# A gated linear attention followed by a SwiGLU: the norm's roots spread over the partitions by way of DRAM, and the column sum of the squares in four column groups

## The chip, the cores and the metric

The kernel runs on one core of a Trainium2 chip. The metric is the device time of one execution in microseconds. The core has TensorE (PE in the profile; its weight loads are shown apart as PEld), VectorE (DVE), ScalarE (ACT), GpSimd (POOL) and SyncE (SP), which here only issues DMAs.

## The reference

Four sequences of 768 steps and eight heads of 48 features go through a recurrent attention with a complex gate (`gateloop`); its output, with the heads side by side as 3072 tokens of 384 features, goes through an RMS norm and a SwiGLU of width 1536.

```python
mag = np.sqrt(a_re * a_re + a_im * a_im)
scale = np.minimum(mag, 0.999) / (mag + 1e-06)
a_re_n, a_im_n = (a_re * scale, a_im * scale)
for t in range(S):
    ar, ai = (a_re_n[:, :, t, :, None], a_im_n[:, :, t, :, None])
    new_re = ar * S_re - ai * S_im
    new_im = ar * S_im + ai * S_re
    kv = np.einsum('bhd,bhe->bhde', k[:, :, t], v[:, :, t])
    S_re, S_im = (new_re + kv, new_im)
    y[:, :, t] = np.einsum('bhd,bhde->bhe', q[:, :, t], S_re)
...
rms = np.sqrt(np.mean(x * x, axis=-1, keepdims=True) + 1e-06)
xn = x / rms * rms_g
g = xn @ w_gate
silu = g * (1.0 / (1.0 + np.exp(-g)))
val = xn @ w_val
return (silu * val @ w_out).astype(np.float32)
```

All data is fp32, and so are all products on TensorE.

## The kernel before

**Tiling.** The 3072 tokens are 24 chunks of C = 128 (n = 0 to 23, six to a sequence). Two chunks make a group (g = 0 to 11) for the feed-forward part. Features lie on the partitions from the attention's output on: `yT` is 3 blocks of 128 features by 128 tokens in one PSUM bank.

**Stages.** `gates(u)` turns the gates of one or two chunks into running products (magnitude and angle) on ScalarE and VectorE and writes the rotated q and k into `rot`; twelve DMAs for two chunks (`kq<-rot`) bring them into the layout `kq`, 96 partitions by head and time. `attend(n)` is the attention of one chunk: score products in column groups of 32 (`bank<-kq`), a masked copy into `am` by VectorE, the products for y (`bank<-am,ve` and `bank<-kq,state`, in column groups too), transposes of k (`bank<-ident,kq`), and the new state (`bank<-vn,kt`, column groups). At its end stands the norm of that chunk. `feed(g, xT)` is the SwiGLU of a group: six pairs of gate and value products (`bank<-xT,wg`, `bank<-xT,wv`, 128x256), ScalarE's Silu into `sg`, VectorE's product into `hT`, and the output products: of 384 columns (`bank<-wo,hT`) for groups 0 and 1, and from group 2 on (`FIRST`) a product of two-by-two blocks with seven instead of eight multiplications, of 192 columns (tiles `wo`, `sums`, `hT`, with sums on VectorE in `mid` and `hT`), into `ot` and by DMA to `out`.

**The norm of a chunk.** ScalarE squares `yT` into `sq`; VectorE multiplies `yT` by the norm's weights into `yg` and adds the three blocks of `sq` into the first (for chunks 0 to 3, whose units are in `LIGHT`, ScalarE does the former, and the three blocks are added by the product). Then, on one column of bank 7:

- the column sum: `sq` as weights, a column of ones as the moving side, so that each token's sum of squares lands on its own partition (`bank<-ones,sq`, 128x1);
- `ssv`: mean and epsilon, on VectorE;
- `rs`: to the power -1/2, on GpSimd (`pow`), 128x1;
- the root product: `rs` widened to 128 columns as weights, the identity as moving side, which puts the 128 roots side by side on every partition (`bank<-ident,rs`, 128x128);
- `xT` = `yg` times that row, on VectorE. `xT` is what the gate and value products of the group read.

**What sets the order.** Every operation is recorded with an estimated duration and what it reads and writes, and `Flow.schedule` makes one list of it: at each step it takes the engine that can start first and on it the ready operation that is due first. Products of the feed-forward part have due times from a running clock; others inherit them from who uses them. A DMA counts as landed 2.0 us after its turn in its queue, and SP has at most eight DMAs under way (`LANES`). A change between products on the whole array and in column groups (`mode=BLK`) counts 0.06 us. Within an engine the order is then fixed; all instructions are issued by one line, L667, so that in the profile groups are told apart by tiles alone. Column groups are seen in the form: `128*128` is the whole array, `128*32` and `96*32` are column groups of 32. One fp32 product of the program leaves two records in the trace.

PSUM: banks 0 to 3 take turns for the feed-forward part, 4 and 5 hold scores and state, 6 holds `yT`, 7 holds the norm's column and row and transposes.

Of the kernel before, what the change touches and what calls it, by code (L numbers as in the profile page):

```python
# [8 lines left out]
FP32 = mybir.dt.float32  # L9
# [7 lines left out]
DRAM = bass.MemoryType.DRAM  # L17

P = 128
C = 128  # L20
BLK = 32
# [440 lines left out]
class Flow:  # L462
# [59 lines left out]
    def add(self, eng, calls, dur, reads=(), writes=(), table=None, land=None, due=None, after=(), behind=(), late=None, mode=None):  # L522
        op = dict(i=len(self.ops), eng=eng, calls=calls, dur=dur, deps=set(), table=table, land=land,
                  base=due, late=late, mode=mode, stage=self.stage, behind={o["i"] for o in behind})
        self.ops.append(op)
        op["deps"].update(o["i"] for o in after)
        for ap in reads:
            self.note(op, ap, False)
        for ap in writes:
            self.note(op, ap, True)  # L530
        return op
# [138 lines left out]
def fast(tc, ctx, qT, kT, v, a_re, a_im, w_gate, w_val, w_out, rms_g, out, H, bad):  # L670
# [6 lines left out]
    N = B * NCH  # L677
# [15 lines left out]

    mem = ctx.enter_context(tc.tile_pool(name="mem", bufs=1))
    psum = ctx.enter_context(tc.tile_pool(name="psum", bufs=1, space=PSUM))
    rooms = {}

    def room(name, shape, dtype=FP32):
        t = mem.tile(shape, dtype, name=name, tag=name)
        row = 1  # L700
        for x in shape[1:]:
            row *= x
        rooms[t.tensor.name] = (name, row * mybir.dt.size(dtype))
        keep.append(t)
        return t

    outside = {x.tensor.name for x in (qT, kT, v, a_re, a_im, w_gate, w_val, w_out, rms_g, out)}
    keep = []
    banks = []
    for i in range(8):  # L710
        t = psum.tile([P, 512], FP32, name=f"bank{i}", tag=f"bank{i}")
# [52 lines left out]
    def act(o, x, func, scale=None, bias=None, accum=None, **kw):  # L764
        k = {}
        if scale is not None:
            k["scale"] = scale
        if bias is not None:
            k["bias"] = bias
        if accum is not None:  # L770
            k["accum_out"] = accum
        dur = 0.17 + 0.86e-3 * cols(o) + 0.09 * len(aps(scale, bias)) + (0.19 if accum is not None else 0.0)
        return add("ACT", [(nc.scalar.activation, (), dict(out=o, in_=x, func=func, **k))], dur,
                   aps(x, scale, bias), aps(o, accum), table=TABLE.get(func), **kw)
# [3 lines left out]
    def run(x):  # L778
        n = 1
        for step, size in reversed([tuple(y) for y in x.ap][0 if x.tensor.name in outside else 1:]):  # L780
            if step != n:
                break
            n *= size
        return n

    def dma(o, x, eng="SP", **kw):
        n = mybir.dt.size(o.dtype)
        for s in o.shape:
            n *= s
        row = mybir.dt.size(o.dtype) * min(run(o), run(x))  # L790
        load = n / row * (0.006 + 50.3e-6 * row) / 16
        op = add(eng, [(QUEUE[eng].dma_start, (), dict(out=o, in_=x))], 0.85 if eng == "POOL" else 0.62, [x], [o],
                 land=2.0 + 1.4 * load, **kw)
        op["load"] = load
        op["packet"] = max(0.07, 0.006 + 50.3e-6 * row * (2 if eng == "POOL" and row == 2048 else 1))
        return op

    def mms(list_, dur, **kw):
        calls, reads, writes = [], [], []
        for o, l, r, start, stop in list_:  # L800
            calls.append((nc.tensor.matmul, (o,), dict(lhsT=l, rhs=r, start=start, stop=stop)))
            reads += [l, r]
            writes.append(o)
        return add("PE", calls, dur, reads, writes, **kw)
# [9 lines left out]
    ident = room("ident", [P, P])  # L814
    causal = room("causal", [C, 2, C])
    mhalf = room("mhalf", [P, 1])
    ones = room("ones", [P, 1])
# [31 lines left out]
    ygs = [room(f"yg{i}", [P, ND, C]) for i in range(2)]  # L849
    ssv = room("ssv", [P, N])  # L850
    rss = [room(f"rs{i}", [P, 1]) for i in range(2)]
    sgs = [room(f"sg{i}", [P, 512]) for i in range(2)]
    ots = [room(f"ot{i}", [C, DM]) for i in range(2)]
    sums = room("sums", [P, 2, HD * DH])
# [106 lines left out]
    EARLY = {0: -100.0, 1: -98.0}  # L961
    SUMMED = ()
    LIGHT = (0, 1, 2)
    turn = {}
    moved = {}
    HOLD = 1
# [134 lines left out]
    def attend(n):  # L1101
# [12 lines left out]
        for a in range(2):  # L1114
            ps = banks[4 + a]
            s = ps.rearrange("s (h t) -> s h t", h=HH)
            list_ = []
            for h in range(HH):
                for b in range(4):
                    c = 3 - b if h % 2 else b  # L1120
# [5 lines left out]
            o = am[:, a * HH:(a + 1) * HH]  # L1126
# [3 lines left out]
        ps = banks[6]  # L1130
# [3 lines left out]
        for i in range(4 * ND):  # L1134
            j, c = divmod(i, 4)
            m, r = divmod(i, 3)
            o = yT[c * BLK:(c + 1) * BLK, j]
# [10 lines left out]
        if not last:  # L1148
            kt = kts[0]
            for a in range(2):  # L1150
                ps = banks[7 - 3 * a]
# [5 lines left out]
            ps = banks[5][0:D2, 0:DM]  # L1157
# [4 lines left out]
            u, i = unit_of[n], n - UNITS[unit_of[n]][0]  # L1162
# [9 lines left out]
        sq, yg = sqs[0], ygs[n % 2]  # L1172
        act(sq, yT, AF.Square)
        if unit_of[n] in LIGHT:
            for j in range(ND):
                act(yg[:, j], yT[:, j], AF.Copy, scale=gcol[:, j:j + 1])
        else:
# [3 lines left out]
        ps = banks[7]  # L1181
        col = ps[:, C:C + 1]
        parts = range(ND if unit_of[n] in LIGHT else 1)
        mms([(col, sq[:, j], ones, j == 0, j == parts[-1]) for j in parts], 0.25 * len(parts))
        sv = ssv[:, n:n + 1]
        ts(sv, col, 1.0 / DM, EPS_RMS, ALU.mult, ALU.add)
        add("POOL", [(nc.gpsimd.tensor_tensor, (), dict(out=rss[n % 2], in0=sv, in1=mhalf,
                                                        op=ALU.pow))], 0.9, [sv, mhalf], [rss[n % 2]])
        wide = ps[:, 0:C]
        mms([(wide, rss[n % 2].to_broadcast([P, P]), ident, True, True)], 0.25)  # L1190
        g = group_of[n]
        ns = GROUPS[g]
        x, lo = xplace[g]
# [2 lines left out]
        i = n - ns[0]  # L1196
# [106 lines left out]
    for n in range(N):  # L1303
        while gated < NU and UNITS[gated][0] <= n:
            gates(gated)
            gated += 1
        xT = attend(n)
        if n == GROUPS[group_of[n]][-1]:
            feed(group_of[n], xT)
            if group_of[n] == 2:  # L1310
                for i in range(len(looks)):
                    look(i)
# [8 lines left out]
    o = 0  # L1321
# [8 lines left out]
    ps = banks[7]  # L1330
# [15 lines left out]
def gateloop_swiglu(tc, qT, kT, v, a_re, a_im, w_gate, w_val, w_out, rms_g, out, H):  # L1346
    nc = tc.nc
    with tc.tile_pool(name="flag", bufs=1) as flag:
        bad = flag.tile([1, 1], I32, name="bad")
        with ExitStack() as ctx:  # L1350
            fast(tc, ctx, qT, kT, v, a_re, a_im, w_gate, w_val, w_out, rms_g, out, H, bad)
        with tc.If(nc.values_load(bad[0:1, 0:1]) > 0):
            general(tc, qT, kT, v, a_re, a_im, w_gate, w_val, w_out, rms_g, out, H)
# [39 lines left out]
```

## Time and profile before

| | |
|---|---|
| time, three runs | 727.68, 730.59, 731.40 us; median 730.59 |
| profiled execution | 729.62 us, span 727.9 us, granted clock 0.99 |
| TensorE busy | 685.7 us (94%), 6906 records |
| VectorE, ScalarE, GpSimd busy | 471.6 (65%), 334.1 (46%), 42.0 us (6%) |
| root products (`bank<-ident,rs`) | 48 records, 10.3 us busy |
| column sums (`bank<-ones,sq`) | 64 records, 9.4 us busy |
| roots on GpSimd (`rs<-ssv,mhalf`) | 24, mean 717 ns |
| xT on VectorE (`xT<-yg,bank`) | 24, mean 547 ns, waited 5.3 us |

The span is from the first to the last instruction of one execution. Busy time of TensorE counts records whose ends are modelled and which overlap, so the mean of a record is longer than its share of the time; the start of one row of the timeline to the start of the next is a better measure. In the page, slices are fortieths of the span, digits tenths; the chain is the work that ended last, followed back from the end.

### The profile page before, as it was taken

How to read it: one execution, taken by the hardware profiler on the slowest of the kernel's cores; microseconds unless marked ns; L12 is line 12 of the kernel's file. 1: busy time of each engine (PE TensorE's matmuls, PEld its weight loads, DVE VectorE, ACT ScalarE, POOL GpSimd, SP SyncE). 2: the span in 40 equal slices, each digit the busy share in tenths (PEclk: the TensorE clock that was granted, in tenths of full speed). 3: DMA queues.
4: the chain of work that ended last, by engine and by line, in shares of the span. 5: the costliest groups of instructions: out<-in, count | busy, mean ns of one | idle time of the engine just before them, and what ended most of it. 6: DMA issues, size and time to landing. Idle time of an engine off the chain costs nothing.

```text
span 727.9 us, 16198 instructions
## 1 busy us (share of the span) xinstructions
PE 685.7 (94%) x6906; PEld 603.7 (83%) x6906; DVE 471.6 (65%) x740; ACT 334.1 (46%) x452; POOL 42.0 (6%) x80
## 2 busy tenths in 40 slices
PE   0579999999999999999999999999999999999996
PEld 0558867877899889889899889889889889889885
DVE  6979988789897887787847737756745234134121
ACT  7649756755656765732923823822821110110010
POOL 6123100001000000000000000000000000000000
PEclk9979999999999999999999999999999999999999
DMA  8797655634545435543722303314303102200000
GB/s 285 226 304 208 193 168 170 184 106 130 170 127 147 153 93 131 171 153 99 189 82 62 97 20 91 97 34 106 81 17 73 55 12 68 65 13 2 23 1 26
DMA packets 104575, 80.64 MB, mean 111 GB/s; under 512 B 42800, under 2 KB 95280, under 8 KB 104496
## 3 DMA queue, kind: packets, MB, share of 16 engines
q1 hardware_dynamic: 100432, 64.99, 32.8%
q0 software_dynamic: 3264, 14.16, 5.5%
q8 instruction: 56, 0.92, 0.5%
q10 hardware_dynamic: 800, 0.39, 0.2%
q14 instruction: 23, 0.19, 0.1%
HBM read 55.84 MB, written 4.72 MB: 83 GB/s over the span
## 4 chain that ended last, share of the span: by engine, by line
PE 87%; DVE 5%; DMA 3%; ACT 2%; SPq 1%; issue 1%; POOL 0%; DVEq 0%; ACTq 0%
PE bank L667 87%; DMA kq<-rot 2%; SPq L667 1%; DVE turns L667 1%; DVE rot L667 1%; DVE wg L667 1%; ACT t L667 1%; DMA in<-in_a_re_dram 1%; ACT turns L667 0%; DVE t L667 0%; DVE wo L667 0%; DVE wv L667 0%; ACT L667 0%; DVE ot L667 0%; DVE in L667 0%
## 5 line engine op out<-in xcount | busy, mean ns | idle before, releaser
L667 PE MATMUL bank<-xT,wg 128*128 128x256 f32 x864 | 199.8, 381 | 1.6 <-DVE xT L667 1.5
L667 PE MATMUL bank<-xT,wv 128*128 128x256 f32 x864 | 199.1, 380 | 0.0
L667 PEld LDWEIGHTS bank<-xT,wg 128*128 128x128 f32 x864 | 163.7, 191 | 24.5 <-DVE xT L667 2.2
L667 PEld LDWEIGHTS bank<-xT,wv 128*128 128x128 f32 x864 | 163.5, 190 | 22.5
L667 PE MATMUL bank<-wo,hT 128*128 128x192 f32 (+1 forms) x576 | 125.8, 362 | 0.4 <-DVE hT L667 0.4
L667 DVE TENSOR_TENSOR hT<-bank,sg 128x512 f32<-128x512 f32 x72 | 49.6, 689 | 114.4 <-PE bank L667 102.0
L667 PEld LDWEIGHTS bank<-wo,hT 128*128 128x128 f32 x576 | 95.6, 191 | 13.7 <-issue 2.5
L667 ACT ACTIVATE sg<-bank 128x512 f32<-128x512 f32 x72 | 42.9, 596 | 132.0 <-PE bank L667 131.4
L667 ACT ACT_TABLE_LOAD x69 | 88.5, 1283 | 11.5 <-DVE rot L667 7.9
L667 ACT ACTIVATE sq<-bank 128x384 f32<-128x384 f32 x24 | 11.8, 490 | 101.2 <-PE bank L667 101.2
L667 DVE TENSOR_TENSOR rot<-kin,turns 128x768 f32<-128x768 f32 x48 | 44.8, 953 | 14.9 <-DMA kq<-rot 14.5
L667 POOL TENSOR_TENSOR rs<-ssv,mhalf 128x1 f32<-128x1 f32 x24 | 17.2, 717 | 575.4 <-DVE ssv L667 575.4
L667 ACT ACTIVATE kt<-bank 128x384 f32<-128x384 f32 x40 | 18.4, 488 | 60.0 <-PE bank L667 59.8
L667 PE MATMUL bank<-sums,hT 128*128 128x192 f32 x240 | 45.0, 329 | 0.0
L667 ACT ACTIVATE turns<-in 128x768 f32<-128x768 f32 (+1 forms) x39 | 29.9, 789 | 21.0 <-DVE rot L667 12.5
L667 PEld LDWEIGHTS bank<-sums,hT 128*128 128x128 f32 x240 | 39.5, 190 | 0.0
L667 PEld LDWEIGHTS bank<-kq 96*32 96x32 f32 x1536 | 30.3, 111 | 10.4 <-issue 7.7
L667 DVE COPY_PREDICATED am<-causal,bank 128x512 f32<-128x512 int32 x48 | 33.3, 722 | 8.4 <-PE bank L667 8.4
L667 DVE TENSOR_TENSOR hT<-hT 128x768 f32<-128x768 f32 x40 | 38.2, 954 | 0.9
L667 PE MATMUL bank<-am,ve 128*32 128x128 f32 x768 | 38.1, 281 | 0.0
L667 PE MATMUL bank<-kq 96*32 96x96 f32 (+3 forms) x1536 | 34.7, 238 | 3.6 <-DMA kq<-rot 3.6
L667 PE MATMUL bank<-rot 128*128 128x128 f32 x64 | 11.7, 342 | 24.8 <-DVE rot L667 24.8
(112 smaller groups left out, 750.5 us busy)
## 6 DMA issues: line engine op xcount, KB each, us to landing
kq<-rot SPq DMA_DIRECT2D x144, 128.0 KB, 2.4
kin<-in_q_dram SPq DMA_DIRECT2D x24, 192.0 KB, 2.8
kin<-in_k_dram SPq DMA_DIRECT2D x24, 192.0 KB, 3.6
wo<-in_w_gate_dram SPq DMA_DIRECT2D x6, 768.0 KB, 4.6
out_dram<-ot SPq DMA_DIRECT2D x24, 192.0 KB, 2.3
wo<-in_w_val_dram SPq DMA_DIRECT2D x6, 768.0 KB, 5.7
wo<-in_w_out_dram SPq DMA_DIRECT2D x6, 768.0 KB, 5.4
in<-in_a_re_dram SPq DMA_DIRECT2D x11, 384.0 KB, 4.6
```

What stands on the lines that cost most here:

```text
L667: fn(*args, **kw)
```

## The change

Two things are changed in the norm. The column sum is cut into four products, each with 32 columns of `sq` as weights, which write 32 partitions each in column groups; in the planner it counts 0.1 us instead of 0.25. For chunks 4 to 21 (`SENT`) the root product is left out: one DMA writes the column `rs` into a line of 128 numbers in DRAM (two such lines take turns), and a second one reads this line into all 128 partitions of a new tile `row` in SBUF (there is one). `xT` is then multiplied by `row` instead of the bank. Chunks 0 to 3, 22 and 23 keep the root product; its estimate in the planner is 0.28 instead of 0.25. Since the planner makes the whole order from such estimates, the order of the other work changes too.

```diff
+    dram = ctx.enter_context(tc.tile_pool(name="dram", bufs=1, space=DRAM))
...
+    lines_ = []
+    for i in range(2):
+        t = dram.tile([1, P], FP32, name=f"line{i}", tag=f"line{i}")
...
+    row = room("row", [P, C])
...
+    SENT = range(4, N - 2)
...
         ps = banks[7]
         col = ps[:, C:C + 1]
         parts = range(ND if unit_of[n] in LIGHT else 1)
-        mms([(col, sq[:, j], ones, j == 0, j == parts[-1]) for j in parts], 0.25 * len(parts))
+        mms([(col[c * BLK:(c + 1) * BLK], sq[:, j, c * BLK:(c + 1) * BLK], ones, j == 0, j == parts[-1])
+             for j in parts for c in range(4)], 0.1 * len(parts), mode=BLK)
         sv = ssv[:, n:n + 1]
         ts(sv, col, 1.0 / DM, EPS_RMS, ALU.mult, ALU.add)
         add("POOL", [(nc.gpsimd.tensor_tensor, (), dict(out=rss[n % 2], in0=sv, in1=mhalf,
                                                         op=ALU.pow))], 0.9, [sv, mhalf], [rss[n % 2]])
-        wide = ps[:, 0:C]
-        mms([(wide, rss[n % 2].to_broadcast([P, P]), ident, True, True)], 0.25)
+        if n in SENT:
+            line = lines_[n % 2]
+            dma(line.rearrange("o t -> t o"), rss[n % 2])
+            wide = row
+            dma(wide, line.to_broadcast([P, C]))
+        else:
+            wide = ps[:, 0:C]
+            mms([(wide, rss[n % 2].to_broadcast([P, P]), ident, True, True)], 0.28)
...
         tt(xT[:, :, i * C:(i + 1) * C], yg, wide.unsqueeze(1).to_broadcast([P, ND, C]))
```

More of the change, by code (lines that the diff above doesn't have):

```diff
@@ L708, in fast @@
     keep = []
+    lines_ = []
+    for i in range(2):
+        t = dram.tile([1, P], FP32, name=f"line{i}", tag=f"line{i}")
+        rooms[t.tensor.name] = (f"line{i}", P * 4)
+        outside.add(t.tensor.name)
+        keep.append(t)
+        lines_.append(t)
     banks = []
```

## The prediction

> **What bounds the kernel now.** I read the page first: busy shares, the span in 40 slices, the chain that ended last.
>
> ```profile
> span 727.9 us, 16198 instructions
> PE 685.7 (94%) x6906; PEld 603.7 (83%) x6906; DVE 471.6 (65%) x740; ACT 334.1 (46%) x452; POOL 42.0 (6%) x80
> ...
> PE   0579999999999999999999999999999999999996
> ...
> PE 87%; DVE 5%; DMA 3%; ACT 2%; SPq 1%; issue 1%; POOL 0%; DVEq 0%; ACTq 0%
> ```
>
> After the first three slices (some 55 us) TensorE never rests, and 87% of the chain is its products. In stretches of 50 us, PE is busy 50.00 us in six of the eleven from 150 to 700 and over 49.1 in the others; its waits over 0.2 us after 120 us are 0.82 (at 324), 0.26 (at 510), 0.89 (at 675) and 0.41 us (at 717), 2.4 together. So here a nanosecond of TensorE is a nanosecond of span, and other engines matter only if they make TensorE wait. Busy time says little of pipelined products, so I price them by starts, in the timeline of PE. A column "x6" counts records; one fp32 product of the program leaves two.
>
> ```profile
> 314.51 0.88 PE L667 MATMUL bank<-vn,kt 128*32 128x48 f32 x48
> 315.30 0.77 PE L667 MATMUL bank<-kq 96*32 96x128 f32 x32
> ...
> 333.72 1.14 PE L667 MATMUL bank<-sums,hT 128*128 128x192 f32 x6
> 334.79 0.43 PE L667 MATMUL bank<-am,ve 128*32 128x128 f32 x8
> 335.03 0.40 PE L667 MATMUL bank<-kq,state 96*32 96x128 f32 x8
> ...
> 336.35 0.40 PE L667 MATMUL bank<-kq,state 96*32 96x128 f32 x8
> 336.69 1.24 PE L667 MATMUL bank<-hT 128*128 128x192 f32 x6
> 337.76 0.38 PE L667 MATMUL bank<-ident,rs 128*128 128x128 f32 x2
> 337.99 1.14 PE L667 MATMUL bank<-wo,hT 128*128 128x192 f32 x6
> 338.96 1.14 PE L667 MATMUL bank<-sums,hT 128*128 128x192 f32 x6
> 339.94 0.28 PE L667 MATMUL bank<-ones,sq 128*128 128x1 f32 x2
> 340.08 1.22 PE L667 MATMUL bank<-sums,hT 128*128 128x192 f32 x6
> 341.14 1.14 PE L667 MATMUL bank<-wo,hT 128*128 128x192 f32 x6
> ```
>
> Four prices stand in these starts. Six records of 192 columns that nothing disturbs take 0.97 us (337.99 to 338.96). **A root product** (ident,rs) takes 0.23 (337.76 to 337.99). **A column sum** (ones,sq) takes 0.14, and the six records behind it 1.06 instead of 0.97: 0.23 here, 0.20 as a mean over all of them; I take 0.21. **A visit to column groups** (from 128*128 to a form in *32 and back) costs time besides its products: the six records before it take 1.07 (+0.10), its first eight 0.24 and its last eight 0.34 where an inner eight take 0.22 (+0.02, +0.12), the six after it 1.07 (+0.10). That is 0.34 here; the same subtraction over all visits between 120 and 715 us gives 0.31, so 0.155 for each change of mode. **A record in column groups** takes 16.5 ns at 48 columns (0.79 us by 48) and 27.5 ns at 128 (0.22 by 8).
>
> **The change, part by part.** The schedule that the program makes for itself is known before it runs: I compared the order of instructions of both kernels on each engine.
>
> *Roots.* 18 of 24 root products go (chunks 4 to 21): 18 x 0.23 = -4.1 us, all on the path.
>
> *Column sums.* Two of the first chunks fall into time in which PE waits anyway and are left out. Before, 20 sums of one part and 2 of three: 26 x 0.21 = 5.4 us. After, a part is four products, 8 records: 26 x 8 = 208 records. No record of the trace moves one column in column groups; the nearest, at 48 columns, is 16.5 ns and falls with the columns, so I take 15: 3.1 us. Ends: 10 ns (2.1) and the 27.5 of 128 columns (5.7). So -2.3, between -3.3 and +0.3.
>
> The Trainium skill, "TensorEngine Tiling (Array Packing)", section Instruction Overhead, speaks against this part: a product of one column lasts as long as one of 60, and a small dimension should not be tiled. At its 60 cycles, 25 ns at 2.4 GHz (an estimate from that page, with the clock of the page "TensorE: Matmul & The Clock Gate"), the part would give -0.2 and not -2.3; the 16.5 ns at 48 columns are already below that, so the row decides.
>
> *Changes of mode.* The order holds 120 changes between the two modes before and 150 after. In 22 of 24 chunks the new sum stands alone between products of the whole array: 44 changes, and 14 fall away because the order is another elsewhere. Without the two visits in the early wait it is 26 x 0.155 = +4.0 us (26 x 0.17 = 4.4 by the visit shown above).
>
> Sum on PE: -4.1 - 2.3 + 4.0 = **-2.4 us**; with the ends of the column price -3.4 and +0.6 (with 4.4 for the mode). A term nearly cancels a term: what the new sums save goes into visits to the other mode, and the gain is about half of what the roots free.
>
> *DMAs.* 36 issues on SP at 0.6 us each (the SPq pieces of the chain in order of time) are 22 us of SP; SP waited 178 us for PE alone, so its time is there, but not its order. The pow of POOL stays. The multiplication into xT reads SBUF for PSUM: state in 96x384 takes 549 ns from SBUF and 550 from PSUM, so nothing. What counts is the latency, and no row shows a column going to DRAM or a row coming back to all partitions. The nearest:
>
> ```profile
> kq<-rot SPq DMA_DIRECT2D x144, 128.0 KB, 2.4
> out_dram<-ot SPq DMA_DIRECT2D x24, 192.0 KB, 2.3
> ve<-in_v_dram SPq DMA_DIRECT2D x96, 24.0 KB, 2.3
> decay<-ends SPq DMA_DIRECT2D x66, 1.0 KB, 1.8
> ```
>
> The last column is the median from issue to landing. decay<-ends also moves a few bytes for each of 128 places, within SBUF: I take its 1.8 us for the column, 2.4 for the row (64 KB, between ve and kq), 4.2 together; ends 3.6 (twice decay) and, by the latest ve (11.9) behind large loads, over 10. The chain from column sum to feed is then 0.15 (ssv) + 0.55 (pow) + 1.8 + 2.4 + 0.55 (xT) + six handovers of 0.05 = 5.8 us; some 1.5 more where DVE or SP is busy. **The cover:** in the new order the second chunk's sum is followed by 18 output products, 8 transposes and 12 output products before the first gate product of its group, 30 x 2 x 0.163 + 1.3 = 11 us, in eight of nine groups. In the group of chunks 4 and 5 it is 12 products of 384 columns and 16 small ones, 8.4 us. So some 4 us of slack remain, 1 to 2.5 in that first group; I put 0 to 1.5 us of wait there and take 0.2. If the cover goes, each microsecond of lateness is one of span for that group.
>
> *New waits.* On DVE, xT of the first chunk waits for `row`; right behind it in most groups stand the second chunk's ssv, the `mid` additions and the evictions of output products. On SP, `line` waits for the pow and `row` for the landing of `line`; behind them stand kq<-rot and decay (score products of the next chunk need them), loads of k, q, v and `out`. Those are issued well ahead: PE waited for kq only 3.6 us, before 101 us. There is one `row`: a second chunk's read waits for the first's xT. Taken as nothing at the prices above.
>
> *Stalls freed.* Of PE's 2.4 us of waits those at 675 and 717 belong to the last group, whose chunks keep the product; 0.82 and 0.26 may go or move: nothing taken, -1.1 as the end.
>
> Sum: -2.4 + 0.2 = **-2.2 us**. The profiled execution took 729.62 us (span 727.9, 1.7 around it), so 727.4; the median of 730.59 is 0.97 above that execution, so 728.4. Half a per cent, about what a measurement of this kernel can tell from no change, is 3.7 us: the forecast lies inside it.
>
> **The rivals.** *The round trip through DRAM becomes the path (slower).* The two DMAs of both chunks of a group stand almost in series, since DVE runs the second ssv behind the first xT. Let each DMA land D later than assumed; a group then loses 4D less its slack, some 5 us with the little that the first chunk has, and there are nine. It decides from D = 1.2: at 1.5 (column 3.3, row 3.9) it is 9 x 1 = +9 us, 736; at 2, +27. For it: the column is 128 pieces of 4 bytes to one place in DRAM, and single DMAs in the trace land after 5 us and more when behind loads of 768 KB on the same queue. Against: decay at 1.8, and in the second half the queues are nearly empty. Chance 0.2. The Trainium skill, "DMA: Bandwidth & Descriptors", section Specifications, says that pieces below 512 B are read, modified and written; no price stands there and no row of this trace shows it for DRAM.
>
> *The column groups cost more than the roots give (slower or even).* If a one-column record takes the 27.5 ns of 128 columns and a visit 0.34, the sum is +0.6; with 2 to 3 us of waits at the feeds +3 to +4, 733 to 734. Chance 0.06.
>
> *The new order frees more than the sum (faster).* Planned further ahead, the attention of a group ends earlier, the waits at 324 and 510 go, and a record costs 10 ns: -3.4 - 1.1 = -4.5, 726; fewer late drains make it up to -6. Chance 0.14.
>
> That the change does nothing of what it says is excluded by the order: 18 root products are gone and 36 DMAs stand on SP.
>
> **How the numbers follow.** The forecast's case, 0.60, runs from -4 to +2 around -2.2: 0.10 of it is faster by over 0.5%, 0.48 within, 0.02 slower. With the rivals: faster 0.10 + 0.14 = 0.24; same 0.48; slower 0.02 + 0.20 + 0.06 = 0.28. The forecast's own range is 726.5 to 732; the whole reaches from 725 (the faster rival's middle and below left out, 0.08) to 738 (D above 1.6 left out, some 0.12).
>
> **What would show it.** Right: 12 records of ident,rs (6 products); 256 of ones,sq (32 parts by 8) in a form *32 with starts 10 to 20 ns apart; 0.3 us lost around each lone sum; `line` landing in about 2 us, `row` in about 2.4; no wait of PE for xT over 0.5 us outside the first and last groups. Wrong: PE waiting for xT in most groups (the DRAM rival), landings over 3 us, starts of 25 ns and more in the sums, or a visit that costs well under or over 0.31.

## The result and the profile after

The changed kernel takes 857.49 us (median of four runs) against 729.94 before: 1.1753 times as long, 95% interval 1.1687 to 1.182. The forecast was 728.4 us with a range to 738. The rival "the round trip through DRAM becomes the path" is what happened: 127.6 us, where it was worked out for 9 (each DMA 1.5 us late) and 27 (2 us late).

The page of the changed kernel, busy time, slices and chain:

```profile
span 852.9 us, 16622 instructions
...
PE 717.7 (84%) x7066; PEld 623.2 (73%) x7066; DVE 471.0 (55%) x740; ACT 330.5 (39%) x449; POOL 46.1 (5%) x80
...
PE   0679899769959968987994997996798799699996
...
PEclk9999999979979989996997998998899799799999
...
PE bank L667 17%; DMA line<-rs 3%; SPq L667 1%; DMA row<-line 1%; DMA kq<-rot 1%; DVE hT L667 0%; DVE ot L667 0%; DVE xT L667 0%; DVE mid L667 0%; DVE ssv L667 0%; DVEq L667 0%
```

Three things are new: TensorE has holes through the whole middle of the run; its granted clock, full after the start before, now dips beside them; and `line<-rs` and `row<-line` stand in the chain. The chain's shares stop at a quarter of the span because it could be followed back no further, so they are not a breakdown. Who waited for whom says more:

```profile
DVE xT L667 <- DMA row<-line: 149.3, 18, 11.3
...
PE bank L667 <- DVE hT L667: 38.8, 9, 9.3
...
PE bank L667 <- DVE ot L667: 24.3, 6, 6.1
```

(total, times, longest.) All 18 rows were waited for, 8.3 us each on VectorE. TensorE waited in turn, and mostly not for `xT` itself (9.9 us in all) but for what stood behind it on VectorE: output evictions (`ot`) and sums for the output products (`hT`). The DMA issues of the changed kernel, KB each and median us from issue to landing:

```profile
kq<-rot SPq DMA_DIRECT2D x144, 128.0 KB, 3.5
...
row<-line SPq DMA_DIRECT2D x18, 64.0 KB, 4.6
...
line<-rs SPq DMA_DIRECT2D x18, 0.5 KB, 7.9
```

The column of 512 bytes takes 7.9 us where 1.8 was assumed, the row 4.6 where 2.4 was: 12.5 for the round trip instead of 4.2. (The page gives a landing for 8 of the columns and 10 of the rows; from the semaphores' updates, as in e4 below, the 18 columns take 6.9 to 9.8 us and the 18 rows 4.0 to 5.4.) `kq<-rot`, at 2.4 us before, lands in 3.5: traffic behind the new DMAs on the queue is later too. By the same updates, a `kq<-rot` issued while a column is under way takes 6.4 us at the median, while a row is under way 4.5, and otherwise still 2.4. One group (chunks 12 and 13) shows how that becomes time. VectorE's timeline (start, us, engine, operation, idle before it and who ended that):

```profile
434.33 0.16 DVE L667 TENSOR_SCALAR ssv<-bank 128x1 f32<-128x1 f32 x1 [0.35 <-PE bank L667]
...
450.14 0.56 DVE L667 TENSOR_TENSOR xT<-yg,row 128x384 f32<-128x384 f32 x1 [9.81 <-DMA row<-line]
450.61 0.15 DVE L667 TENSOR_SCALAR ssv<-bank 128x1 f32<-128x1 f32 x1
...
463.87 0.56 DVE L667 TENSOR_TENSOR xT<-yg,row 128x384 f32<-128x384 f32 x1 [8.89 <-DMA row<-line]
...
466.20 0.55 DVE L667 TENSOR_TENSOR ot<-bank,mid 128x384 f32<-128x384 f32 x1
```

SyncE's in the same stretch:

```profile
437.20 0.53 SPq L667 DMA_DIRECT2D line<-rs  x1
...
445.28 0.33 SPq L667 DMA_DIRECT2D row<-line  x1
...
451.66 0.33 SPq L667 DMA_DIRECT2D line<-rs  x1
...
458.62 0.33 SPq L667 DMA_DIRECT2D row<-line  x1
```

And TensorE's:

```profile
450.82 0.55 PE L667 MATMUL bank<-ident,kq 96*128 96x96 f32 x4 [3.44 <-DVE ssv L667]
454.50 2.29 PE L667 MATMUL bank<-wo,hT 128*128 128x192 f32 x6 [3.13 <-DVE hT L667]
...
466.81 1.65 PE L667 MATMUL bank<-xT,wg 128*128 128x256 f32 x3 [6.09 <-DVE ot L667]
```

The two round trips are in series, as the rival said: the second chunk's column sum was done on TensorE at 441, but its `ssv` stands behind the first `xT` on VectorE (450.61), so the second column goes out at 451.66. Between 447 and 467 TensorE loses 12.7 us in these three waits. The first product after them, a transpose into bank 7, waits for `ssv` because it needs the bank that `ssv` reads. The wait at 466.81 is put down to `ot` (466.20), but that itself stood behind xT.

Busy time of the engines from 120 us to the end, the changed kernel and then the kernel before (window, length, PE, PEld, DVE, ACT, POOL, clock, DMA share, GB/s):

```profile
120.00:852.90 732.90, 633.56 (x6032) 554.84 (x6030) 368.46 (x595) 247.89 (x329) 16.81 (x20) 0.93 0.29 75
```

```profile
120.00:727.90 607.90, 598.79 (x5958) 532.81 (x5957) 369.84 (x598) 253.16 (x333) 13.66 (x20) 1.00 0.32 88
```

The 125.0 us longer stretch is made of waits of TensorE over 0.2 us (92.6 in all against 2.4: +90.2) and of busy time (+34.8). The second part is the clock, 0.93 instead of 1.00 for nearly the same work. In the trace the granted clock is either full or half; busy TensorE time after 120 us that falls into stretches of half clock loses 38.0 us of full speed, enough for the 34.8. In this group it reads, changed kernel:

```profile
450.00:467.00 17.00, 6.96 (x29) 6.48 (x30) 7.83 (x18) 2.74 (x4) 0.74 (x1) 0.76 0.24 54
467.00:485.00 18.00, 18.00 (x72) 15.41 (x73) 8.75 (x11) 13.37 (x16) 0.00 (x0) 0.85 0.28 85
```

The clock is at half from 451.9 to 458.7 and from 465.5 to 472.3. Behind the last wait, the first 12 records of 256 columns take 440 ns each (466.81 to 472.09), and those from 474.81 on take 216, the undisturbed rate: a wait of TensorE costs itself and then some of what follows. Over the run that is 34.8 by 90.2, 0.39 us more for each microsecond waited. The Trainium skill, "TensorE: Matmul & The Clock Gate", section "HAM oscillation — how this bites in real kernels", has the rule that pauses over some 3.4 us bring the slow clock back; the waits of 3.1 to 6.1 us in this group, with a clock of 0.76 and 0.85 around them, agree. Shorter waits can do it too: in e7 below, one of 2.17 us is followed by 3.4 us at half clock and one of 2.01 us is not, and in e8, whose waits end at 1.75 us, none is.

### The profile page after: what moved, and what is told of

It is laid out like the page before. It is cut to its first block, busy times and chain, and to the rows that moved or that the text cites. A ratio compares the mean times of both kernels' runs of the same rounds, so it can differ in the third digit from the quotient of the medians.

```text
span 852.9 us, 16622 instructions
## 1 busy us (share of the span) xinstructions
PE 717.7 (84%) x7066; PEld 623.2 (73%) x7066; DVE 471.0 (55%) x740; ACT 330.5 (39%) x449; POOL 46.1 (5%) x80
## 5 line engine op out<-in xcount | busy, mean ns | idle before, releaser
L667 PE MATMUL bank<-xT,wg 128*128 128x256 f32 x864 | 211.4, 397 | 31.0 <-DVE ot L667 24.3
L667 PEld LDWEIGHTS bank<-xT,wg 128*128 128x128 f32 x864 | 171.1, 200 | 58.1 <-DVE ot L667 26.1
L667 PE MATMUL bank<-wo,hT 128*128 128x192 f32 (+1 forms) x576 | 134.3, 382 | 38.8 <-DVE hT L667 38.8
L667 PEld LDWEIGHTS bank<-wo,hT 128*128 128x128 f32 x576 | 103.0, 204 | 54.3 <-DVE hT L667 40.6
L667 DVE TENSOR_TENSOR xT<-yg,row 128x384 f32<-128x384 f32 x18 | 10.0, 558 | 149.3 <-DMA row<-line 149.3
L667 POOL TENSOR_TENSOR rs<-ssv,mhalf 128x1 f32<-128x1 f32 x24 | 20.4, 851 | 695.5 <-DVE ssv L667 589.3
L667 PE MATMUL bank<-sums,hT 128*128 128x192 f32 x240 | 57.3, 395 | 0.0
L667 ACT ACTIVATE t<-t 128x768 f32<-128x768 f32 (+1 forms) x39 | 30.9, 791 | 60.7 <-DVE t L667 60.2
L667 PEld LDWEIGHTS bank<-sums,hT 128*128 128x128 f32 x240 | 53.4, 243 | 0.0
L667 PE MATMUL bank<-kq 96*32 96x32 f32 (+3 forms) x1536 | 35.7, 236 | 7.6 <-issue 4.7
```

The costliest lines, as they stand in the source:

```text
L667: fn(*args, **kw)
```

## Experiments

Theory 1: the round trip's latency, not covered by the order that was planned with some 4.5 us for it, makes nearly all of the loss. Theory 2: the visits to column groups cost far more than priced. Theory 3: the DMAs as such (issues on SP, traffic held up) cost, whatever waits for them.

**e1_cols: the column groups alone** (the root product's estimate stays at the changed 0.28).

```diff
-    SENT = range(4, N - 2)
+    SENT = ()
```

> Only the column sum in four column groups; all 24 roots by product, no DMA. Theory 1 (the round trip through DRAM makes nearly all of the loss: TensorE waits for it, and after each wait runs at a lower clock): the order has 148 changes of mode for 120, so 24 x 0.155 = +3.7 us outside the early wait, sums 5.4 -> 3.1 us by 15 ns a record or 4.5 by the 21.6 ns that the trace of the changed kernel shows; together +1.4 to +2.8 us, some 731.5 to 733. Theory 2 (the visits to column groups cost far more than priced): 760 or more. No wait of TensorE over 1 us in the middle of the run by either.

Measured: 1.0001 times before (0.9973 to 1.0029), 729.87 us. Theory 2 falls: this half of the change is worth nothing that can be told, between -2.0 and +2.1 us. A lone sum in PE's timeline:

```profile
332.87 1.14 PE L667 MATMUL bank<-sums,hT 128*128 128x192 f32 x6
333.94 0.24 PE L667 MATMUL bank<-ones,sq 128*32 128x1 f32 x8
334.11 1.24 PE L667 MATMUL bank<-hT 128*128 128x192 f32 x6
335.19 1.14 PE L667 MATMUL bank<-sums,hT 128*128 128x192 f32 x6
```

The six before it take 1.07, the sum 0.17, the six after it 1.08 instead of 0.97: 0.38 us in all where the product on the whole array cost 0.21. Where it is followed by other column groups (at 167.73), the eight records take 0.085 us, 10.6 ns each. So the record is cheap, and a lone visit costs more than the sum saves. In the trace TensorE's busy time after 120 us is 1.9 us longer than before (600.7 for 598.8) and its waits are 0.8 us shorter, which the noise of the times covers.

**e2_dram: the trip through DRAM alone**, the column sum as before.

> Only the trip through DRAM for chunks 4 to 21; the column sum stays one product on the whole array. Theory 1: 845 to 860 us, waits of TensorE of 85 to 100 us in all, column landing near 7.9 us and row near 4.6. Theory 2: near 735, since the visits are gone.

Measured: 1.1872 (1.1776 to 1.1969), 869.35 us; TensorE's waits over 0.2 us after 120 us 105.8, column 8.1, row 4.8. The whole loss is in this half; it is 9 us over the upper end of what was expected, with more waits than the 85 to 100 us.

**e3_told: the same kernel, the planner told the truth.**

```diff
-            dma(line.rearrange("o t -> t o"), rss[n % 2])
+            dma(line.rearrange("o t -> t o"), rss[n % 2], lag=5.8)
...
-            dma(wide, line.to_broadcast([P, C]))
+            dma(wide, line.to_broadcast([P, C]), lag=2.3)
```

(`lag` is added to a DMA's landing in `Flow.schedule` and in the due times.)

> The changed kernel; only the planner is told 5.8 us more for the column's DMA and 2.3 us more for the row's, as measured, so that it puts more of other work between. Theory 1, latency without cover: the waits of TensorE fall from 92 us to 10 to 20, their cost in clock with them, 735 to 750 us. Theory 3 (the small DMAs hold up the queue, and other loads behind them come late, whatever the order): stays over 800.

Measured: 1.0517 (1.0451 to 1.0583), 765.21 us; waits of TensorE 26.2 instead of 92.6. Seven tenths of the loss go when the order is planned for the latency, against theory 3 as it was put. More stays than expected (15 us over the upper end), and it is mostly not the row: VectorE waits 12.5 us for rows instead of 149.3. TensorE's two longest waits, 8.48 and 5.36 us, stand behind VectorE waiting 10.51 us for a load of weights (`wo<-in_w_val_dram`, landed after 13.4 us) and 5.79 us for `kq<-rot`, both issued while a column was under way. e11 takes this up.

**e4_writes: the column's DMA by itself, in six forms**, in the kernel before, where nothing waits for it.

```diff
+            to, x = ((far["wline"].rearrange("o t -> t o"), r), (far["wnear"][:, 0:1], r), (far["wfar"][:, 0:1], r),
+                     (inner, r), (far["wsixteen"], yg[:, 0, 0:16]), (far["wfull"], yg[:, 0]))[n % 6]
+            dma(to, x)
```

> The kernel before, all roots by product; in chunks 4 to 21 one more DMA each that nobody waits for, in six forms, three of each: 128 pieces of 4 bytes side by side in DRAM (as in the change), 4 bytes every 64 bytes, 4 bytes every 512 bytes, 4 bytes side by side on one partition of SBUF, 64 bytes side by side in DRAM, 512 bytes side by side. If DRAM's handling of pieces that share a small stretch is what takes the time, only the first lands in 7 to 8 us and the others in 2 to 3; if it is 4 byte pieces into DRAM, the first three do; if it is pieces of any size or where they come from, all but the last two. Time: within 1% of before if waiting is what costs (theory 1); over 800 if the DMAs hold up other traffic (theory 3).

Measured: 730.31 us in one run (before: 729.22), so these 18 DMAs cost nothing that one run can tell while nobody waits. Only three of them have the form of the change, too few to test theory 3. The profile lists a landing for two of the forms only, so I took it from the trace as the last of the sixteen updates of a DMA's semaphore before that semaphore's next DMA:

| form, 128 pieces each | landings, us |
|---|---|
| 4 bytes side by side in DRAM (the change) | 9.5, 9.7 (the third has 7 of 16 updates recorded) |
| 4 bytes, every 64 bytes of DRAM | 2.0, 2.6, 3.7 |
| 4 bytes, every 512 bytes of DRAM | 1.6, 1.7, 3.6 |
| 4 bytes side by side on one partition of SBUF | 1.9, 2.1, 4.4 |
| 64 bytes side by side in DRAM | 1.6, 1.9, 2.4 |
| 512 bytes side by side in DRAM | 1.8, 2.0, 3.2 |

Neither the 4 bytes nor DRAM alone make it slow, but only both with many pieces in the same 64 bytes; distances between 4 and 64 bytes were not run. The Trainium skill, "DMA: Bandwidth & Descriptors", section Specifications, puts the read-modify-write below 512 bytes; here single 4 byte pieces that lie apart land as fast as pieces of 512 bytes, and those that share a stretch are slow. That the sharers wait for each other's read and write is my inference.

**e5_reads: the row's DMA by itself**, 64 KB into 128 partitions in four forms.

> The kernel before, all roots by product; in chunks 4 to 21 one more DMA each that nobody waits for: 64 KB into 128 partitions, in four forms, four or five of each: one DRAM row of 512 bytes read by all partitions (as in the change), 128 different DRAM rows, 128 different SBUF rows, one SBUF partition's row read for all partitions. If the 4.5 us of the row in the changed kernel come from all pieces reading one place in DRAM, the first lands in 4 to 5 us and the second in 2 to 2.5; if it comes from the reads queuing behind the column's write, all four land in 2 to 2.5 here. Time: that of before within 1%.

```profile
gotone<-rline SPq DMA_DIRECT2D x5, 64.0 KB, 4.9
gotone<-rows SPq DMA_DIRECT2D x5, 64.0 KB, 1.9
```

One DRAM row for all partitions lands in 4.9 us, 128 different rows in 1.9. All these DMAs ran before 160 us, beside heavy loading, since nothing tied them to their chunks: single ones took 3.1 to 15.5 and 1.9 to 3.6. The two SBUF forms have one name in the trace; by the order of issue, which repeats the four forms, 128 different SBUF rows took 2.2 to 7.7 us and one SBUF partition's row 3.9 to 7.3, so beside that loading no difference is shown. The run took 735.14 us, 0.9% over before in a single run; whether that is the DMAs in the crowded first stretch is open.

**e6_sbuf: the line in SBUF instead of DRAM**, everything else as in the change.

```diff
-            line = lines_[n % 2]
-            dma(line.rearrange("o t -> t o"), rss[n % 2])
+            line = ok[0:1, 0:C]
+            dma(line, rss[n % 2])
             wide = row
-            dma(wide, line.to_broadcast([P, C]))
+            dma(wide, line.unsqueeze(1).to_broadcast([1, P, C]))
```

> The changed kernel with one thing else: the line of 128 roots lies on one partition of SBUF (in a tile that is free until the end) and not in DRAM; the row is read from there. Column sums in column groups as in the change. Theory 1 (the handling of 4 byte pieces that share 64 bytes of DRAM makes the loss): the column lands in 2.1 us, the loss of 17% goes; with a row of 2.4 us the forecast of the change should hold, -2 us against before, 142 changes of mode taken; with a row of 4.6 us some 5 to 10 us of waits, 732 to 740. If it were the number of hops or of DMAs on SP that costs (theory 3), it stays over 800.

Measured: 1.0175 (1.0147 to 1.0203), 741.66 us, just over the upper end. Nine tenths of the loss go when the line leaves DRAM: the column lands in 2.1 us instead of 7.9, the row in 4.1 instead of 4.6, so most of it is the column of shared pieces. **e7_sbuf_whole**, the same with the sum on the whole array:

> As the one before, with the column sum as one product on the whole array. 118 changes of mode instead of 142 save 3.7 us, the sums cost 2 more: 1 to 2 us under the one before; with a row of 2.4 us -4 us against the kernel before, 725 to 727; with a row of 4.6 us 730 to 738.

Measured: 1.0153 (1.0128 to 1.0178), 739.55 us, 1.6 over the upper end of 730 to 738. Its DMAs:

```profile
row<-ok SPq DMA_DIRECT2D x18, 64.0 KB, 4.0
ok<-rs SPq DMA_DIRECT2D x18, 0.5 KB, 2.0
```

The column is now what I had assumed (2.0 for 1.8), the row is not (4.0 for 2.4). That one place read 128 times is slow in SBUF as well is likely, since `kq<-rot`, 128 KB from SBUF to SBUF, lands in 2.4 here, but e5 does not show it. TensorE still waits 14.6 us, in pieces of at most 2.2 us. So even with DMAs 1.8 us over the assumption together, the planned cover is too thin. The column groups are worth 2 us here, in the direction of the expectation, with intervals that overlap.

**e8_sbuf_told, e9_sbuf_told_more: cover for the SBUF line**, sum on the whole array, a change of mode counted at 0.155 us.

```diff
-                dur += 0.06
+                dur += 0.155
...
+            dma(line, rss[n % 2], lag=0.3)
...
+            dma(wide, line.unsqueeze(1).to_broadcast([1, P, C]), lag=1.7)
```

(3.5 instead of 1.7 in the second.)

> The kernel with the line in SBUF and the sum on the whole array, with the planner told 0.3 us more for the column and 1.7 us more for the row, as measured (2.0 and 4.0 from issue to landing), and 0.155 us for a change of mode. If the rest of the loss is cover alone (theory 1), the 14.6 us of TensorE's waits fall under 5 and the time to 726 to 731, that is within 0.5% of before or just under it. If VectorE standing in order behind the row costs whatever the planner knows, 735 and more.

Measured: 1.003 (1.0005 to 1.0054), 733.76 us; waits 5.6 us. Both are over what was expected of theory 1 (726 to 731, under 5) and under the other reading (735 and more).

> The same with 3.5 us more for the row instead of 1.7, twice the lateness that was measured: more cover than the DMA needs. Theory 1: as the one before within 2 us, a little better if waits in SP's order are what is left.

Measured: **0.9939 (0.9911 to 0.9967), 726.46 us: faster than before.** Waits of TensorE over 0.2 us after 120 us: 0.6. VectorE before xT (idle time ended by, us, times):

```profile
DMA row<-ok: 2.9, 3
```

From ssv to xT the chain takes 10.8 us at the median here and 9.5 in e7: it isn't shorter, it is only no longer waited for. Lateness told exactly isn't enough; the same DMAs with twice the row's lateness are hidden. The gap between the two medians is 7 us (9 between the profiled executions), of which the waits explain 5.0; the rest stays open.

**e10_mode: the control.** The kernel before with a change of mode at 0.155 us.

> The kernel before with one number in its planner: a change of mode counts 0.155 us instead of 0.06. The control for the two others: 115 changes instead of 120 and other places for the same work; 727 to 730, no difference that can be told.

Measured: 1.0001 (0.9978 to 1.0024). The gain of e9 isn't that number's.

**e11_dram_told_more: the same cover for DRAM.**

> The counterpart of the last SBUF kernel with the line in DRAM again: sum on the whole array, a change of mode counted at 0.155 us, the planner told 8.0 us more for the column and 4.5 us more for the row, each about 2.2 us more than measured. If cover is all that it takes, it comes out at 726 to 731 as the SBUF kernel did. If 12.5 us for two chunks of a group in turn, over one line and one row, are more than a group has to put over them, waits of 10 us and more stay: 738 to 760.

Measured: 1.0363 (1.0315 to 1.0412), 752.68 us; waits 18.7 us, from ssv to xT 19.7 us at the median. The time lies in the range that was given for a trip too long to be covered, but by luck: the trip is covered. VectorE waits for none of the 18 rows. TensorE's two longest waits, 6.61 and 3.98 us, have another cause; the second, by VectorE's and TensorE's timelines:

```profile
403.67 0.95 DVE L667 TENSOR_REDUCE small<-wo 128x1 f32<-128x768 f32 x1 [7.86 <-DMA wo<-in_w_out_dram]
...
405.27 3.56 PE L667 MATMUL bank<-wo,hT 128*128 128x192 f32 x12 [3.98 <-DVE hT L667]
```

`small` is a reduction over weights just loaded. Their load was issued at 392.75, behind a column issued at 392.09, and landed after 10.9 us; the other one like it landed after 11.0 us. The loads of `wo<-in_w_out_dram` that no column was ahead of landed in 5.1 at the median, and small DMAs show the same: `ve<-in_v_dram` takes 7.2 us behind a column and 2.6 otherwise. So theory 3 is right for a part. Once the trip is covered, the slow column still costs, because the queue's other traffic lands late behind it; with the column in SBUF (e9) no load is held so. What this part is worth in time was not run by itself.

## Why the prediction was wrong

**What held.** TensorE was the bound. The 18 root products and the changes of mode stand in the order as counted. The record of one column costs 10.6 ns, next to the low end (10), not 15; the page's 60 cycles, which I charged to each record, are not seen there, though by product (two records, 21 ns) they nearly are. The sum on PE, -2.4 us, agrees with what e1 shows of its column half (0 with 2 us either way). That the roots' half pays was seen only when the trip was hidden: e9 gains 0.6%.

**The step that failed: the price of the two DMAs.** "I take its 1.8 us for the column, 2.4 for the row ..., 4.2 together". It measured 7.9 and 4.6. The nearest rows were nearest in bytes and pieces, but not in the thing that decides, where the pieces go: decay's 128 small pieces go into SBUF, where e4 finds even 128 side by side on one partition landed in 1.9 to 4.4, the column's all to 512 bytes of DRAM in a row, and ve's and kq's pieces come from different places, the row's all from one. The text had the sign of it ("128 pieces of 4 bytes to one place in DRAM") and left it at a chance of 0.2; the end "over 10" of the bounds never reached the range, which stopped at D = 1.6 (D is how much later than assumed each DMA lands). By the text's own formula D = 1.6 would give 12.6 us, about 740, and not the 738 at which the range ends. Measured D is half of (7.9 - 1.8) + (4.6 - 2.4), 4.15.

**The rival's formula.** 9 x (4D - 5) gives 9 x 11.6 = +104 us at that D, against 90 us of new waits: near in size, since the two trips of a group are in series. Two things were missing. "If the cover goes, each microsecond of lateness is one of span": it is 1.39, by the clock (34.8 us). And no one slack fits: 90.2 us over nine groups leave 6.6 us of slack, but at D = 0.9 (e7: 2.0 and 4.0) the formula gives no wait, and 14.6 us were measured, 12.2 more than before, which leaves 2.2. I had counted cover on TensorE from the column sum to the feed; what binds earlier is VectorE's order, where `ssv`, `mid` and `ot` of the same group, and in e7 the additions into `sq`, stand behind `xT`. "Taken as nothing at the prices above" was the sentence to distrust: a wait put into an in-order engine needs its own slack, at the place where it stands. The same sentence covers `kq<-rot` and the loads behind the new DMAs on SP, which land late behind a column (e3, e11).

**The new order.** That cover was planned for about 4.5 us is why neither 12.5 nor 6 were hidden. e9 shows that cover alone hides the trip through SBUF; e3 and e11 show that cover hides the trip through DRAM from VectorE, and leave the traffic held up behind the column.

**A reading.** TensorE is busy 50.00 us in seven of the eleven stretches of 50 us from 150 to 700, not in six; nothing rests on it.

## What to carry to other kernels

A DMA's price is read from a row that is like it in where the pieces lie, not only in how many and how big they are: before trading a product of 0.23 us for a trip through memory, measure that trip as a bystander in the kernel as it is. When a scheduler orders in-order engines by estimated latencies, an estimate that is too short turns into waits on every engine behind it; here the lateness told had to exceed the measured one by about 2 us before the waits for the row went (e9, e11). A slow DMA also delays what is issued behind it on its queue, which an estimate of its own landing does not cover. Where TensorE is the bound, price its long waits above one for one: 1.39 here, while in e7, whose waits stay under 2.2 us, the granted clock from 120 us on is still 1.00.

## What the runs showed of the hardware

128 pieces of 4 bytes into one row of 512 bytes of DRAM land in 7 to 10 us; spread to every 64 bytes, in 2.0 to 3.7; on one partition of SBUF, in 1.9 to 4.4. While such a DRAM column is under way, DMAs issued behind it on the queue land late: `kq<-rot` in 6.4 us for 2.4 (the changed kernel), `ve<-in_v_dram` in 7.2 for 2.6 (e11). A row of 512 bytes read by all 128 partitions lands in 4.6 us from DRAM and 4.0 from one partition of SBUF, 128 different rows of DRAM in 1.9. Around waits of 3.1 to 6.1 us TensorE's granted clock is at half for 6.8 us at a time, 0.76 and 0.85 over stretches of 17 and 18 us; over the changed kernel that costs 0.39 us for each one waited.
